# T5-bias attention and a gated adapter layer on one core: loads without a cast, regrouped exps, and a PV tile by head

## The chip, the cores and the metric

The kernel runs on one core of one Trainium2 chip. The metric is device time in microseconds (us) of one execution; lower is better. A core has a matrix engine (PE), whose weight loads are shown as a row of their own (PEld), a vector engine (DVE), a scalar engine for exps (ACT), a general engine (POOL, in code `nc.gpsimd`) and a queue processor (SP, in code `nc.sync`) that here issues transfers (DMAs). Each engine works through its own list of instructions in order; between engines there are semaphore waits. PE writes its results into PSUM, a small memory of eight banks of 2 KB on each of 128 partitions; DVE and ACT read it from there into SBUF, the working memory.

## The reference

Batch 8, 8 heads, 576 tokens, 64 numbers a head. All inputs are f32.

```
scores = q k^T / 8 + bias_table[bucket(|i - j|), head]
attn   = softmax(scores) ;  x = attn v            # x: 4608 tokens x 512
logits = x w_gate                                 # 8 adapters
w      = softmax over the two largest logits
out    = x + sum over these two:  w_e (x A_e) B_e  # A_e 512x16, B_e 16x512
```

The bucket depends on the distance alone and is the last one (31) from distance 128 on.

## The kernel before

**Tokens.** 576 tokens are four blocks of 128 and a tail of 64. Two heads make a pair; there are 8 batches x 4 pairs = 32 pairs, and the main loop (L502) runs over them with five steps g in each. Scores are computed transposed: keys on the partitions, queries along the row. Steps g = 0 to 3 take 128 keys each, for both heads; step 4 takes the 64 tail keys of both heads together.

**Loads.** `load` (L66), `load_tails` and `load_v` issue DMAs from POOL; the source is f32 and the destination bf16, so the transfer itself casts. At the first pair of a batch (L505 to L508) all of the next batch's k and q are asked for, at the second pair its v. The waits for a free buffer stand in POOL's list, as do the memsets of `vts`, `vns` and `tlTs` (L177 to L182, L219 to L222).

**Bias.** Softmax is unchanged by a constant, so the table is taken relative to its last entry, and exp(score + bias) is exp(score) times exp(bias). The factor differs from 1 only where |i - j| < 128. L117 to L149 build exp(bias) as one row per head (`ge`), write it to DRAM, and read it back shifted by one for each partition (`Mr`, `MHr`, L150 to L164); `bias_pair` (L171) copies it reversed into `M` and `MH`. `band` (L278) multiplies the part of the exps near the diagonal with it, on DVE.

**One pair.** `transposes` (L228) puts the pair's k and q through PE and copies them out of PSUM (`kqT`, one DVE copy of 1024 columns); at a batch's first pair also the tails (`tlT`). `qk` (L253) makes 1024 columns of scores for the four query blocks and two heads, and 128 for the tail queries, in three PSUM banks; `softmax_exp` (L272) takes the exp of all 1152 columns in one instruction (640 in step 4). One step later in the list, `pv_main` (L295) and `pv_rest` (L316) multiply the previous pair's exps with v, which has a column of ones so that the sum of exps comes out beside the result: three query blocks in one PSUM tile (`pvA`), the fourth and the tails in another (`pvB`). `norm_main` and `norm_rest` (L341 to L362) divide, on DVE. In the tail rows of `pvB` each half holds one head's queries against both heads' v; `mask` zeroes the half that does not belong.

**The adapter layer.** When a batch's four pairs are done, `pieces` (L477) puts its work into a queue: transposes of x (`m_x`, and `m_xtail` for the tails of two batches together), logits and gates (`m_gate`), x A (`m_z`), its transpose (`m_zT`), the product with B plus x (`m_out`, `m_outt`) and the stores, issued from SP. The main loop takes one piece at the steps 0, 3 and 4 of each pair.

**Order.** It is written out by hand: `manual_schedule` (L54) keeps each engine's instructions in program order. PSUM has two tiles of three banks for scores (`scp`) and two of one bank for all else (`acp`).

The softmax here doesn't subtract the row's maximum and nothing guards it: scores larger than these inputs give would overflow.

## Time and profile before

| | us |
|---|---|
| runs: median (lowest to highest, two runs) | 260.19 (259.83 to 260.55) |
| profiled execution: span, first to last instruction | 257.7 |
| what lies around the span, by the median | 2.5 |
| first exp of the scores starts | 28.63 |
| third pair's first exp starts | 41.20 |
| last pair's first exp starts | 233.96 |
| last exp of the scores starts | 238.37 |

The profile is of one execution. Its page gives each engine's busy time, then the span in 40 slices with the busy tenths of each engine; the trace behind it answers by group of instructions, by tile, by wait and by stretch of time. A group's row reads: line, engine, operation, output <- inputs, shapes, count, then busy time in all and mean ns of one, then the engine's idle time just before them. A row of waits reads: who waited, at which line, for whom, the sum in us, how often, the longest.

### The profile page before, as it was taken

The numbers are of one execution on the slowest core, as the hardware profiler recorded it, in microseconds if no ns is written. First come the engines' busy times: TensorE is split into PE (matmuls) and PEld (weight loads), VectorE is DVE, ScalarE is ACT, GpSimd is POOL, SyncE is SP. The second block draws the span as 40 slices with busy tenths as digits, with TensorE's granted clock in tenths as the row PEclk, the third lists the DMA queues.
The fourth block names the chain that finished last, engine by engine and source line by source line (L and its number), as shares of the span: only waits on it lengthen the run. The fifth ranks groups of instructions, "written<-read, shape, count | busy, mean of one in ns | idle before, by whom it ended". The sixth has DMA issues, their size and how long they took to land.

```text
span 257.7 us, 6522 instructions
## 1 busy us (share of the span) xinstructions
PE 189.7 (74%) x2576; PEld 120.1 (47%) x2576; DVE 205.9 (80%) x641; ACT 165.4 (64%) x174; POOL 117.3 (46%) x155
## 2 busy tenths in 40 slices
PE   0020698797878868897799778987898788888852
PEld 0010255465545655456356554564465544664710
DVE  3200678999898888999979898989998889989972
ACT  2000469897769767886688677867796678868100
POOL 8997999745733591185508560549052000000000
PEclk9999999999999999999889999999999999999965
DMA  4999999969893999399939992799969003202205
GB/s 27 141 154 153 94 131 114 137 42 99 85 201 54 105 84 84 122 146 85 163 95 107 58 142 34 133 166 101 147 109 69 0 3 123 84 3 83 85 21 183
DMA packets 124759, 25.56 MB, mean 99 GB/s; under 512 B 118960, under 2 KB 119992, under 8 KB 124728
## 3 DMA queue, kind: packets, MB, share of 16 engines
q0 software_dynamic: 112768, 14.16, 89.6%
q1 hardware_dynamic: 11960, 10.97, 14.6%
q8 instruction: 20, 0.33, 0.5%
q14 instruction: 11, 0.09, 0.1%
HBM read 29.84 MB, written 9.45 MB: 152 GB/s over the span
## 4 chain that ended last, share of the span: by engine, by line
DVE 50%; PE 26%; ACT 7%; POOL 6%; issue 5%; DMA 3%; ACTq 0%; POOLq 0%; DVEq 0%
PE pvA L310 11%; DVE x L348 6%; PE sc L262 5%; DVE x L360 3%; DVE kqT L250 3%; DMA vn_86<-in_v_dram 3%; DVE o L457 3%; DVE xT L377 3%; PE pvA L304 2%; PE kqps L247 2%; DVE rcA L347 2%; POOL qn L69 2%; DVE rmB L358 2%; PE sc L258 1%; PE dl L455 1%
## 5 line engine op out<-in xcount | busy, mean ns | idle before, releaser
L262 PE MATMUL sc<-kqT 64*128 64x512 bf16 x256 | 51.8, 402 | 0.0
L69 POOL DMA_DIRECT2D kn<-in_k_dram x36 | 31.2, 896 | 19.1 <-PE kqps L247 18.2
L69 POOL DMA_DIRECT2D qn<-in_q_dram x36 | 31.0, 906 | 1.6 <-DMA vn_86<-in_v_dram 1.5
L258 PE MATMUL sc<-tlT_184,kqT 128*128 128x128 bf16 x64 | 14.5, 226 | 18.3 <-DVE kqT L250 13.0
L69 POOL DMA_DIRECT2D vn_87<-in_v_dram x16 | 14.0, 894 | 28.4 <-PE pvB L336 28.4
L69 POOL DMA_DIRECT2D vn_86<-in_v_dram x16 | 14.0, 896 | 27.7 <-PE pvB L336 27.6
L262 PEld LDWEIGHTS <-kqT 64*128 64x128 bf16 x256 | 12.4, 93 | 26.5 <-issue 17.4
L250 DVE COPY kqT<-kqps 128x1024 bf16<-128x1024 bf16 x32 | 21.8, 683 | 3.5 <-PE kqps L247 3.4
L457 DVE TENSOR_TENSOR o<-dl,x 128x512 f32<-128x512 f32 x32 | 21.8, 683 | 1.6 <-DMA out_dram<-o 0.8
L258 PEld LDWEIGHTS <-kqT 128*128 128x128 bf16 x128 | 12.8, 100 | 17.7 <-DVE kqT L250 13.2
L348 DVE TENSOR_TENSOR x<-pvA,rcA 128x384 bf16<-128x384 f32 x32 | 17.8, 557 | 1.1
L455 PE MATMUL dl<-Bb,zT 128*128 128x512 bf16 x32 | 13.3, 421 | 6.8 <-DVE zT L449 2.8
L275 ACT ACTIVATE p_227<-sc 128x1152 bf16<-128x1152 f32 x1 | 1.1, 1131 | 23.4 <-PE sc L262 23.4
L239 DVE COPY tlT_184<-tps 64x512 bf16<-64x512 bf16 x8 | 3.4, 419 | 15.4 <-POOL tlT_184 L221 15.3
L258 PE MATMUL sc<-tlT_186,kqT 128*128 128x128 bf16 x64 | 14.2, 222 | 1.7 <-ACT p_571 L275 0.7
L360 DVE TENSOR_TENSOR x<-pvB,rmB 128x256 bf16<-128x256 f32 x32 | 13.6, 424 | 1.1
L347 DVE RECIPROCAL rcA<-pvA 128x6 f32<-128x6 f32 x32 | 6.2, 195 | 10.1 <-PE pvA L304 9.9
L247 PE MATMUL kqps<-ident,kn 128*128 128x128 bf16 x128 | 13.3, 229 | 1.0 <-DVE o L457 0.6
L412 ACT ACTIVATE ex<-df 128x32 f32<-128x32 f32 (+1 forms) x12 | 2.7, 222 | 17.0 <-DVE df L409 17.0
L234 PE MATMUL tps<-ident,tl 128*128 128x128 bf16 x32 | 3.4, 232 | 13.3 <-DMA tl<-in_q_dram 13.3
L247 PE MATMUL kqps<-ident,qn 128*128 128x128 bf16 x128 | 13.1, 228 | 0.0
L247 PEld LDWEIGHTS <-kn 128*128 128x128 bf16 x128 | 8.2, 101 | 7.5 <-issue 6.8
(1431 smaller groups left out, 655.4 us busy)
## 6 DMA issues: line engine op xcount, KB each, us to landing
out_dram<-o SPq DMA_DIRECT2D x32, 256.0 KB, 2.1
kn<-in_k_dram POOLq DMA_DIRECT2D x28, 128.0 KB, 4.1
qn<-in_q_dram POOLq DMA_DIRECT2D x28, 128.0 KB, 4.7
vn_86<-in_v_dram POOLq DMA_DIRECT2D x16, 128.0 KB, 5.1
vn_87<-in_v_dram POOLq DMA_DIRECT2D x16, 128.0 KB, 4.4
out_dram<-o SPq DMA_DIRECT2D x8, 128.0 KB, 4.6
Mr<-g_d SPq DMA_DIRECT2D x1, 576.0 KB, 6.6
tl<-in_k_dram POOLq DMA_DIRECT2D x8, 64.0 KB, 4.0
```

The lines of the kernel that those rows point to most:

```text
L69: nc.gpsimd.dma_start(out=o, in_=src[b, h0:h1, j * 128:(j + 1) * 128, :] .rearrange("h p d -> p h d"))
L247: nc.tensor.transpose(ps[:, w, j * 128:(j + 1) * 128], n[:, j, 2 * hp:2 * hp + 2, :], ident)
L250: nc.vector.tensor_copy(t, ps)
L258: nc.tensor.matmul(sc[:, 1024:1152], lhsT=t[:, 0, g * 128:(g + 1) * 128], rhs=tt[:, hp, 1, :], start=True, stop=True)
L262: nc.tensor.matmul(sc[:, h * 512:(h + 1) * 512], lhsT=t[s, 0, g * 128:(g + 1) * 128], rhs=t[s, 1, :], start=True, stop=True)
L310: nc.tensor.matmul(acc[:, qb, h, :], lhsT=p[:, o:o + 128], rhs=vn[:, g, 2 * hp + h, :], start=first, stop=False, skip_group_check=True)
L347: nc.vector.reciprocal(rc, acc[:, :, :, D])
L348: nc.vector.tensor_tensor(x[:, 0:3, 2 * hp:2 * hp + 2, :], acc[:, :, :, :D], rc.unsqueeze(3).to_broadcast((128, 3, 2, D)), op=ALU.mult)
L360: nc.vector.tensor_tensor(x[:, 3:5, 2 * hp:2 * hp + 2, :], acc[:, :, :, :D], rm.unsqueeze(3).to_broadcast((128, 2, 2, D)), op=ALU.mult)
L377: nc.vector.tensor_copy(xT[:, :, half * 256:(half + 1) * 256], ps)
L455: nc.tensor.matmul(ps, lhsT=zT[:, t, :], rhs=Bb, start=True, stop=True)
L457: nc.vector.tensor_tensor(o, ps, xs[b][:, t].rearrange("p h d -> p (h d)"), op=ALU.add)
```

## The change

- **Loads** come per pair, in f32, from SP, without a cast: two for k, one for q, two for v. Up to four pairs are asked for ahead. The first pair's q and the bias table are issued from ACT.
- **q** is laid out so that partition p holds tokens 4p to 4p + 3, which makes one run of 1 KB. Query column (j, p) of a tile is now token 4p + j; the output's rows are stored by the same rule. So a key block's band covers 64 or 96 columns in each of the four groups j, and `M` is built with a step of 4.
- **Casts** to bf16 are instructions of POOL (`cast_kq`, `cast_v`, `cast_tail`, `cast_vtail`); for the first pair k and the tails are cast on DVE and q on ACT.
- **Exp groups** are 1024 columns in two banks. The fifth group of a pair holds the tail queries against the four key blocks and the tail keys against the four query blocks; tail queries against tail keys are done once a batch for all four pairs (`tails_sc`, `tails_band`).
- **PV** uses one tile of two banks, one head in each, filled in six parts; it is normalized in one go (`norm`). A third tile pool (`misc_ps`) takes everything else.
- **The order**: scores are issued one group ahead of their exp and the band follows one group behind it; gating is cut into three pieces, `m_z` into two, `m_xtail` runs for each batch; pieces carry weights, and each step of a pair has a budget.

```diff
-    def load(dst, src, b, h0, h1, cols=None):
-        for j in range(4):
-            o = dst[:, j, h0:h1, :D]
-            nc.gpsimd.dma_start(
-                out=o, in_=src[b, h0:h1, j * 128:(j + 1) * 128, :]
-                .rearrange("h p d -> p h d"))
...
+    def load_nat(t, s, i, e):
+        b, hp = divmod(i, HP)
+        for h in range(2):
+            e.dma_start(out=t[:, :, h, :], in_=s[b, 2 * hp + h, 0:S4, :]
+                        .rearrange("(g p) d -> p g d", p=128))
+
+    def load(i, e0=None, e1=None):
+        b, hp = divmod(i, HP)
+        kf = ldp.tile([128, 4, 2, D], FP32, name="kf", tag="kf")
+        qf = ldp.tile([128, 2, 256], FP32, name="qf", tag="qf")
+        load_nat(kf, k, i, e0 or SY)
+        (e1 or SY).dma_start(out=qf, in_=q[b, 2 * hp:2 * hp + 2, 0:S4, :]
+                             .rearrange("h (p j) d -> p h (j d)", j=4))
+        stg[i] = [kf, qf, None]
...
+    def cast_kq(i, e0=None, e1=None):
+        kb = ntp.tile([128, 4, 2, D], BF16, name="kb", tag="kb")
+        qb = ntp.tile([128, 4, 2, D], BF16, name="qb", tag="qb")
+        copy_on(e0 or PL, kb, stg[i][0])
+        copy_on(e1 or PL, qb, stg[i][1].rearrange("p h (j d) -> p j h d", j=4))
+        kq[i] = (kb, qb)
+
+    def cast_v(i, e=None):
+        vn = vns[i % 4]
+        copy_on(e or PL, vn[:, :, :, 0:D], stg[i][2])
...
+    load(0, SY, AC)
     load_tails(0)
...
+    cast_kq(0, DVE, AC)
+    cast_tail(0, DVE)
+    for t in tlTs:
+        PL.memset(t, 0.0)
...
+    M = cp.tile([128, H, 4, 96], BF16, tag="M")
+    MT = cp.tile([128, H, 64], BF16, tag="MT")
+    MH = cp.tile([128, HP, 4, 32], BF16, tag="MH")
+    MHT = cp.tile([128, HP, 2, 64], BF16, tag="MHT")
...
+    def bias_pair(hp, e):
+        e.tensor_copy(M[:, 2 * hp:2 * hp + 2],
+                      rev(Mr, 2 * hp, 383, [[MW, 2], [-1, 4], [-4, 96]]))
...
+    load(1)
     load_v(0)
-    load_kq(0, 2, H)
...
+    load_vtails(0)
+    load_bias(2, H)
+    load_v(1)
+    load(2)
+    load_v(2)
+    load(3)
+    load_v(3)
...
         else:
-            nc.tensor.matmul(sc[:, 0:512], lhsT=tt[:, hp, 0, :], rhs=t[:, 1, :],
+            for g in range(4):
+                nc.tensor.matmul(sc[:, g * 128:(g + 1) * 128],
+                                 lhsT=t[:, 0, g * 128:(g + 1) * 128],
+                                 rhs=tt[:, hp, 1, :], start=(g == 0), stop=True,
+                                 skip_group_check=True)
+            nc.tensor.matmul(sc[:, 512:1024], lhsT=tt[:, hp, 0, :], rhs=t[:, 1, :],
                              start=True, stop=True)
...
+        pm = p.rearrange("p (h j q) -> p h j q", h=2, j=4)[:, :, :, q0:q1]
+        DVE.tensor_tensor(pm, pm, M[:, 2 * hp:2 * hp + 2, :, x0:x0 + q1 - q0],
+                          op=ALU.mult)
...
+        if part == 0:
+            a = acp.tile([128, 2, S4], FP32, name="pv", tag="pv")
+            st[(i, "acc")] = a[:, :, 0:5 * D1].rearrange("p h (s d) -> p h s d", s=5)
...
+        rc = sp.tile([128, 2, 5], FP32, name="rc", tag="rc")
+        DVE.reciprocal(rc, acc[:, :, :, D])
+        DVE.tensor_tensor(x[:, :, 2 * hp:2 * hp + 2, :].rearrange("p s h d -> p h s d"),
+                          acc[:, :, :, :D],
+                          rc.unsqueeze(3).to_broadcast((128, 2, 5, D)), op=ALU.mult)
...
+    BUD = (.6, .1, .2, .1, .2)
     for i in range(NPAIR + 1):
         b, hp = divmod(i, HP)
...
+        live = i < NPAIR
+        for c in range(5):
+            nxt = (i, c + 1) if c < 4 else (i + 1, 0)
+            if live:
+                if nxt[0] < NPAIR:
+                    sc[nxt] = qk(*nxt)
+                softmax_exp(i, c, sc.pop((i, c)))
+            prev = (i, c - 1) if c else (i - 1, 4)
...
+            if i < HP and c == 1:
+                bias_pair(i, DVE)
+            if (0, 0) <= prev and prev[0] < NPAIR and (live or c == 0):
+                band(*prev)
+            if live:
+                if c == 0:
+                    if i + 4 < NPAIR:
+                        load(i + 4)
+                    if i + 2 < NPAIR:
+                        cast_kq(i + 2)
...
+            if i > 0:
+                for pt in {1: (0, 1), 2: (2,), 3: (3, 4), 4: (5,)}.get(c, ()):
+                    pv(i - 1, pt)
+            if c == 2 and i + 1 < NPAIR:
                 transposes(i + 1)
-            if g == 1 and i > 0:
-                acc = pv_main(i - 1)
-                norm_main(i - 1, acc)
-            if g == 2 and i > 0:
-                acc = pv_rest(i - 1)
-                norm_rest(i - 1, acc)
+            if i > 0 and c == 4:
+                norm(i - 1)
                 if i % HP == 0:
                     queue += pieces(i // HP - 1)
-            if g in (0, 3, 4) and i > 0 and queue:
-                queue.pop(0)()
...
```

## The prediction

> **What bounds the kernel now.** I read the head of the page first, then the busy time of each engine between two marks, then the waits.

> ```profile
> span 257.7 us, 6522 instructions
> ...
> PE 189.7 (74%) x2576; PEld 120.1 (47%) x2576; DVE 205.9 (80%) x641; ACT 165.4 (64%) x174; POOL 117.3 (46%) x155
> ...
> DVE  3200678999898888999979898989998889989972
> ...
> ```

> The marks are the first exp of the third pair (41.20) and of the last pair (233.96). Busy times by engine between them:

> ```profile
> 41.20:234.00 192.80, 162.37 (x2305) 104.61 (x2304) 174.29 (x537) 148.16 (x156) 79.36 (x97) 0.99 1.01 95
> ```

> The columns are PE, weight loads, DVE, ACT, POOL, granted clock, DMA share, GB/s. This is 29 pairs at 6.65 us, and DVE works 174.29/29 = 6.01 us of each. It is the engine that sets the pace; ACT needs 5.11 of it. The list of waits says what fills the other 0.64, and what the first 28.6 us are:

> ```profile
> DVE rcA L347 <- PE pvA L304: 9.9, 25, 1.4
> ...
> ACT p_227 L275 <- PE sc L262: 23.4, 1, 23.4
> ...
> DVE tlT_184 L239 <- POOL tlT_184 L221: 15.3, 1, 15.3
> ```

> At the start, DVE waits 15.3 us for a memset of `tlT` that stands in POOL's queue behind the loads' issues, with the operands' transposes done at 14.8 (the timeline). So the time is 41.2 (to the third pair) + 192.8 + 23.7 (last pair's own exps and the serial end) = 257.7; the median of the runs is 260.19, 2.5 above the span, which I add at the end.

> **The change part by part.**

> *The start.* POOL no longer issues loads, so the memset is early. What is late next, in order: SP issues four loads from 0.74 (about 0.5 each), and the last, the tails, lands 4.0 later (the row of `tl`): 7. DVE casts them (at most 0.68, its time for 512 f32), then runs the ladder of bias copies, now behind that cast: 2.2 us of rows (0.48, 0.23, 0.34, 0.27, 1.22 less overlap), 9.9. Three `tlT` copies (1.28), `kqT` (0.68), scores (0.6): first exp near 12.5, where it was 28.6. The bias table goes on: exp (0.63), write out (1.44, from 5.25 to 6.69 in the timeline), so `Mr` is asked for at 12. SP holds every later load behind this wait and the two `MHr` issues (1.34): pair 1's loads start at 13.8 and land at 18, two casts (0.66 each), transposes, copy and scores (1.9) give pair 1 at 21. Ten issues and then pair 2's own three, at 0.55, end at 21; landing, casts and the same 1.9 give pair 2's first exp near 27.5. Before: 41.2. DVE stands at the first `M` copy until `Mr` lands (12 + 3.9 = 15.9); behind it in its queue is only work that needs pair 1's operands, so this costs nothing. Gain 13.7; if loads land in 2.3 (the 32 KB row) pair 2 starts at 25, if in 6.6 (`Mr`'s) at 32.

> *Norm.* One tile for both heads: five instructions become two.

> ```profile
> L348 DVE TENSOR_TENSOR x<-pvA,rcA 128x384 bf16<-128x384 f32 x32 | 17.8, 557 | 1.1
> L360 DVE TENSOR_TENSOR x<-pvB,rmB 128x256 bf16<-128x256 f32 x32 | 13.6, 424 | 1.1
> L347 DVE RECIPROCAL rcA<-pvA 128x6 f32<-128x6 f32 x32 | 6.2, 195 | 10.1 <-PE pvA L304 9.9
> L356 DVE RECIPROCAL rcB<-pvB 128x4 f32<-128x4 f32 x32 | 5.6, 176 | 0.2
> L358 DVE TENSOR_TENSOR rmB<-rcB,mask 128x4 f32<-128x4 f32 x32 | 5.2, 162 | 1.1
> ```

> Read the means: 195 + 557 + 176 + 162 + 424 = 1514 ns a pair. From 256 to 384 elements costs 133 ns, so 640 take 424 + 3 x 133 = 824, and ten reciprocals 235: 1059. **-0.455 us a pair.**

> *Bands.* The same elements in six instructions: 413 + 549 + 549 + 413 + 2 x 215 = 2.35, where the three lines took (55.72 + 6.29 + 8.15)/29 = 2.42: -0.07. The tails of four pairs are multiplied in one 512-element operation: +0.41/4 = +0.10.

> *Gating.* `m_xtail` runs for each batch with two 256-element copies (285 each, between the 213 and 424 rows) in place of one of 679 per two batches: +0.06 a pair. `m_z` in halves: 2 x 424 for 680, +0.04. The rest is the same. DVE then has 6.01 - 0.455 - 0.07 + 0.10 + 0.06 + 0.04 = **5.69 us a pair**. The bias tables, now read with a step of 4, cost four copies of 0.75 (the 768-element `MH` copy took 0.72) for 0.5 and three of 512 elements (0.42 to 0.68) for 0.95: +2 us, once.

> *POOL casts beside DVE.* Per pair three casts of 512 elements (0.60 to 0.66, the weight casts) and a quarter of three for the tails: 3.75 casts, 2.3 us. POOL has room; the question is DVE. The timeline holds one meeting:

> ```profile
> 36.40 0.60 POOL L214 CAST Bb<-B_f 128x512 bf16<-128x512 f32 x1
> 36.49 0.80 DVE L289 TENSOR_TENSOR p_282<-p_282,M 128x512 bf16<-128x512 bf16 x1
> ```

> The band took 796 ns, not 413: it ran until 0.29 after the cast's end. Hence 0.38 a meeting. Bounds: nothing, and every cast meets a band, 3.75 x 0.38 = 1.43 a pair. Bands are 39% of DVE's work, so I take 0.39 x 1.43 = 0.55, less what falls in time that DVE would idle: **+0.4**. [...]

> *Exp groups.* Starts of successive exps lie 1.02 apart at 1152 columns and 0.72 at 640, so 1024 columns take 0.91; five and a quarter of a 512-column one: 4.7 us a pair where it was 4.8. It hides under DVE as before.

> *PE.* 50 PV matmuls a pair for 41; 24 of them in a row took 0.71 us (120.50 to 121.21), so +0.27, less about as much in scores. PE waits for ACT and DVE now and has cover for it. Scores are issued one group ahead and bands one group late, so that DVE should find its operands ready: of 0.64 idle (0.33 of it for PV) I leave **0.2**; bounds 0 and 0.64.

> *Loads.* Per pair SP issues 5 loads, a tail load and 1.2 stores. A load may wait for the one eight before it, and stores wait for DVE with later loads behind them, but loads run four pairs ahead. Prices:

> ```profile
> L206 SPq DMA_DIRECT2D A_f<-in_moe_A_dram x4: 540/1414/2413, 9.2 to 14.5; - x4
> ...
> L460 SPq DMA_DIRECT2D out_dram<-o x32: 327/332/356, 67.4 to 252.9; - x32
> ```

> A load with 512 rows of 256 B lies between a store of 128 rows (0.33) and the quickest `A_f` with 1024 (0.54): 6 x 0.5 + 1.2 x 0.35 = 3.4 us a pair, under 6.3. Bytes: 0.86 MB in, 0.29 out in 6.3 us, 183 GB/s; between 9 and 16 us the trace moved 185. [...] No row here shows such plain loads. [...]

> *The sum.* Pair: 5.69 + 0.4 + 0.2 = 6.3. Span: 27.5 + 29 x 6.3 + 2 + 23.5 (the end: one norm after all of PV, +0.7, no wait for an output buffer, -0.8) = 235.7; plus 2.5: **238**.

> **Rivals.**

> 1. *Little contention* (22%): POOL's casts, released by transposes and PV, fall beside DVE's PSUM copies. Pair 5.8, start 26: 26 + 168 + 2 + 23 + 2.5 = 222. For it: POOL busy only a third. Against: DVE has few gaps to absorb a meeting.
> 2. *Each cast meets a band* (10%): pair 5.69 + 1.43 + 0.1 = 7.2, 264; the start pays for the loss and no change can be told.
> 3. *The load queue becomes the bound* (9%), the slower case. Its place is SP: if an issue takes `A_f`'s 1.41 us, as with a full queue, 6 x 1.41 + 0.4 = 8.9 us a pair, and 27.5 + 258 + 2 + 23.5 + 2.5 = 313. It decides from 7.07 us a pair, that is 1.1 us per load. For it: `A_f` itself, and 8 loads in flight at most, which at 4.5 us each is 0.56 a load. Against: those issues shared the engines with POOL's packets (89.6% of 16 engines' span), which go away.
> 4. *Only the start is gained* (14%): handoffs between PE, ACT and DVE keep the pair at 6.65: 27.5 + 193 + 2 + 23.5 + 2.5 = 248.

> **How the numbers follow.** The forecast, 230 to 246, has 45%. Range 220 to 258: it takes in cases 1 and 4, about half of case 2's weight beyond the upper end and most of case 3 stay out. A change of 2% (5.2 us) is about what can be told here: faster is below 255. Forecast, 1 and 4 and a little of 2: 0.83; same 0.08; slower 0.09.

> **What would show it.** First exp near 12 to 14 and the third pair's near 27; DVE busy 5.7 to 6.2 a pair with the norm at about 825 ns; some bands at 0.7 to 1.0 us wherever a POOL cast overlaps, 413 or 549 elsewhere; SP never the last releaser of a cast after the first four pairs. Wrong if POOL's casts wait for DMA in the middle, if plain 256 B loads land late, if bands with runs of 64 or 96 elements are slower than before, or if PE holds ACT while waiting for a gating copy.

## The result and the profile after

The changed kernel takes **272.0 us** (271.94 to 272.05) where the kernel before took 260.2: a ratio of **1.047** (95% interval 1.040 to 1.053). It is slower by 4.7%; the forecast was 238, with a range up to 258. The profiled execution took 271.94 with a span of 270.1. Times are medians of all executions of a kernel, while ratios leave out executions more than 1.5% above the fastest of the same kernel, so the two do not always divide exactly.

The head of the page of the changed kernel, with the busy times and the slices of DVE and of the granted clock:

```profile
span 270.1 us, 7307 instructions
...
PE 200.9 (74%) x2872; PEld 139.5 (52%) x2872; DVE 210.2 (78%) x568; ACT 163.8 (61%) x183; POOL 79.6 (29%) x143
...
DVE  1537745887797989896989879898988699869772
...
PEclk9999975997999899986999689988999599979955
```

DVE's total rose by 4 us although 73 of its instructions are gone, and its share of the span fell: more work and more waiting. The last row is new. This is the same row of the kernel before:

```profile
PEclk9999999999999999999889999999999999999965
```

There the clock of PE stood at 9 (90% or more of full speed) nearly throughout the loop; in the changed kernel a notch of 5 to 8 returns about once a batch. The first slices of this row are not readings: the trace has no clock record before 38.3 us (before) and 30.6 us (changed), and up to there two score matmuls take 0.61 us, later, at the full clock, 0.39. So PE ran slow at the start of both kernels although the row shows 9.

To compare like with like I take 24 pairs, from the first exp of the fifth pair to that of the 29th. Busy times by engine between these marks, first of the kernel before, then of the changed one (columns as in the prediction: PE, weight loads, DVE, ACT, POOL, clock, DMA share, GB/s):

```profile
52.56:213.71 161.15, 136.06 (x1929) 87.52 (x1929) 145.24 (x453) 122.61 (x130) 70.47 (x86) 0.99 1.04 97
```

```profile
47.52:221.71 174.19, 141.92 (x2155) 101.36 (x2155) 151.07 (x400) 120.91 (x136) 56.00 (x93) 0.91 0.61 158
```

Divided by 24, a pair took 6.71 us before and takes 7.26 now; DVE works 6.05 and 6.29 of it and is idle 0.66 and 0.96. The span against the sum of the prediction:

| stretch | predicted | measured | difference |
|---|---|---|---|
| start to the third pair's first exp | 27.5 | 28.8 | +1.3 |
| third and fourth pair, with the bias tables | 14.6 | 18.8 | +4.2 |
| 24 pairs | 151.2 | 174.2 | +23.0 |
| 29th to 31st pair | 18.9 | 22.6 | +3.7 |
| from the last pair's first exp | 23.5 | 25.8 | +2.3 |
| span | 235.7 | 270.1 | +34.4 |

Of the 23.0, 151.07 - 24 x 6.09 = 4.9 are DVE's work, and the other 18.1 its idle time, 0.96 a pair where 0.2 was written down.

Who waits, in the list of waits of the changed kernel over the whole span (waiting engine and line, releaser, us in all, times, longest), ACT first:

```profile
ACT p L321 <- PE sc L306: 30.7, 34, 7.2
ACT p L321 <- PE sc L315: 26.9, 19, 4.0
ACT ex L441 <- DVE df L431: 25.3, 12, 7.2
```

```profile
PE sc L306 <- ACT p L321: 19.5, 12, 3.5
PE xps L392 <- DVE x L379: 8.3, 8, 1.2
...
PE tps L264 <- POOL tl L115: 6.5, 1, 6.5
PE dl L489 <- DVE zT L483: 4.1, 5, 1.0
PE kqps L292 <- POOL kb L115: 3.9, 2, 2.8
```

ACT's wait for `df` in the kernel before, between 52 and 234 us:

```profile
ACT ex L412 <- DVE df L409: 10.3, 10, 1.3
```

`ex` is the gating exp. It waits for DVE's `df` (17.7 us of the 25.3 fall between 47.5 and 244), which stands behind a norm and the logits' copy in DVE's list; the exps of the scores are queued behind it on ACT, and PE finds no free score buffer. The timeline at one such place shows both sides, ACT and then PE (start, us, engine, line, operation, how often, and in brackets the idle time before it):

```profile
148.24 0.23 ACT L441 ACTIVATE ex<-df 128x32 f32<-128x32 f32 x1 [1.75 <-DVE df L431]
150.21 0.21 ACT L441 ACTIVATE ex<-df 128x8 f32<-128x8 f32 x1 [1.74 <-DVE df L431]
150.33 1.92 ACT L321 ACTIVATE p<-sc 128x1024 bf16<-128x1024 f32 x2
```

```profile
146.54 0.39 PE L306 MATMUL sc<-kqT 64*128 64x512 bf16 x2
147.21 0.65 PE L351 MATMUL pv<-vn,p 128*128 128x65 bf16 x16 [0.27 <-DVE lg L426]
151.38 0.61 PE L306 MATMUL sc<-kqT 64*128 64x512 bf16 x2 [3.52 <-ACT p L321]
```

PE stands 3.52 us, and after it the same two score matmuls take 0.61 us instead of 0.39. Two stretches of 6.8 us, by window, show the clock in and behind this place:

```profile
150.10:156.90 6.80, 5.52 (x58) 4.27 (x58) 4.54 (x16) 4.24 (x6) 2.40 (x4) 0.50 0.63 150
156.90:163.70 6.80, 6.31 (x102) 4.36 (x99) 6.38 (x16) 5.18 (x6) 1.99 (x3) 1.00 0.01 4
```

The granted clock was 0.50 in the first and 1.00 in the second: 58 matmuls against 102, and DVE worked 4.54 us against 6.38. Part of that is its wait for PE: the `rc` of a norm waited 1.65 us for PE's `pv`, until 157.2.

The fourth pair has a wait of its own. SP's queue and PE in the timeline:

```profile
27.70 4.04 SPq L244 DMA_DIRECT2D A_f<-in_moe_A_dram  x4
...
32.95 1.07 SPq L76 DMA_DIRECT2D vf<-in_v_dram  x2
```

```profile
41.77 0.61 PE L264 MATMUL tps<-ident,tl 128*128 128x128 bf16 x4 [6.48 <-POOL tl L115]
```

The weights' issues stand in SP's list ahead of the tail loads of batch 1, which are issued only at 36.9 and 37.6; POOL's cast of them ends at 41.7, and PE has stood at their transposes since 35.3, with all later scores behind. ACT waited 7.16 us.

### The profile page after: what moved, and what is told of

Same layout as the page of the kernel before. It is cut to its first block, busy times and chain, and to the rows that moved or that the text cites. A ratio compares the mean times of both kernels' runs of the same rounds, so it can differ in the third digit from the quotient of the medians.

```text
span 270.1 us, 7307 instructions
## 1 busy us (share of the span) xinstructions
PE 200.9 (74%) x2872; PEld 139.5 (52%) x2872; DVE 210.2 (78%) x568; ACT 163.8 (61%) x183; POOL 79.6 (29%) x143
## 4 chain that ended last, share of the span: by engine, by line
PE 42%; DVE 36%; issue 5%; SPq 5%; ACT 5%; DMA 4%; POOL 1%; ACTq 0%; DVEq 0%; POOLq 0%
PE pv L351 9%; PE sc L306 9%; DVE p L336 7%; DVE x L379 7%; PE kqps L292 5%; ACT p L321 4%; DVE o L491 4%; DVE kqT L295 3%; PE pv L367 3%; SPq L76 3%; PE xps L392 3%; DMA tf<-in_q_dram 3%; DVE rc L378 2%; PE zp L464 2%; PE pv L359 2%
## 5 line engine op out<-in xcount | busy, mean ns | idle before, releaser
L321 ACT ACTIVATE p<-sc 128x1024 bf16<-128x1024 f32 x160 | 155.3, 1023 | 61.3 <-PE sc L306 30.7
L306 PE MATMUL sc<-kqT 64*128 64x512 bf16 x256 | 54.6, 423 | 22.4 <-ACT p L321 19.5
L336 DVE TENSOR_TENSOR p<-p,M 128x512 bf16<-128x512 bf16 (+1 forms) x128 | 65.7, 545 | 1.1 <-ACT p L321 0.2
L351 PEld LDWEIGHTS <-p 128*128 128x128 bf16 x1024 | 44.1, 104 | 24.2 <-issue 12.8
L351 PE MATMUL pv<-vn,p 128*128 128x65 bf16 x1024 | 52.3, 203 | 4.0 <-DVE x L379 2.9
L115 POOL CAST kb<-kf 128x512 bf16<-128x512 f32 x31 | 21.1, 680 | 85.8 <-PE kqps L292 38.2
L295 DVE COPY kqT<-kqps 128x1024 bf16<-128x1024 bf16 x32 | 22.0, 687 | 14.5 <-PE kqps L292 13.8
L379 DVE TENSOR_TENSOR x<-pv,rc 128x640 bf16<-128x640 f32 x32 | 26.4, 824 | 1.1
L115 POOL CAST vn<-vf 128x512 bf16<-128x512 f32 x32 | 20.9, 654 | 16.0 <-PE pv L359 15.1
L115 POOL CAST qb<-qf 128x512 bf16<-128x512 f32 x31 | 20.5, 660 | 3.0 <-DMA qf<-in_q_dram 2.3
L441 ACT ACTIVATE ex<-df 128x32 f32<-128x32 f32 (+1 forms) x12 | 2.7, 222 | 25.3 <-DVE df L431 25.3
L292 PE MATMUL kqps<-ident,kb 128*128 128x128 bf16 x128 | 14.8, 249 | 3.9 <-POOL kb L115 3.9
L378 DVE RECIPROCAL rc<-pv 128x10 f32<-128x10 f32 x32 | 6.9, 217 | 10.8 <-PE pv L367 10.6
L292 PE MATMUL kqps<-ident,qb 128*128 128x128 bf16 x128 | 15.0, 251 | 0.3 <-POOL qb L115 0.2
L359 PE MATMUL pv<-vn,p 128*128 128x65 bf16 x256 | 14.7, 203 | 0.0
```

Source lines behind the costliest of these rows:

```text
L115: e.tensor_copy(o, i)
L292: nc.tensor.transpose(ps[:, w, j * 128:(j + 1) * 128], kq[i][w][:, j], ident)
L295: DVE.tensor_copy(t, ps)
L306: nc.tensor.matmul(sc[:, h * 512:(h + 1) * 512], lhsT=t[s, 0, c * 128:(c + 1) * 128], rhs=t[s, 1, :], start=True, stop=True)
L321: AC.activation(p, sc, ACT.Exp, scale=scale)
L336: DVE.tensor_tensor(pm, pm, M[:, 2 * hp:2 * hp + 2, :, x0:x0 + q1 - q0], op=ALU.mult)
```

## The experiments

Three suspects, then: **A**, the wait for the gating exp, with the clock that falls behind it; **B**, POOL's casts, which lengthen DVE's work; and the tails behind the weights. Ratios are to the kernel before, run beside each. Kernels with half-speed stretches scatter between executions (e6 from 256.4 us at a clock of 0.938 to 263.6 at 0.901), and each profile is of one of them: 263.3 us in e5, 261.5 in e6 and 244.5 in e11, above the median, and 265.8, 264.1 and 276.3 in e1, e2 and e3, below it. So a difference of about 0.1 us between two pairs of this table tells nothing: the loops of e1 and e5 differ only in where the weights are cast, and their pairs are 7.07 and 7.18.

| | casts | gating exp | PE filled | pair | DVE busy | DVE idle | PE busy | clock | ratio (95%) |
|---|---|---|---|---|---|---|---|---|---|
| before | in the DMA | same step | | 6.71 | 6.05 | 0.66 | 5.67 | 0.99 | 1 |
| after | POOL | same step | | 7.26 | 6.29 | 0.96 | 5.91 | 0.91 | 1.047 (1.040 to 1.053) |
| e1 | POOL | later | | 7.07 | 6.34 | 0.72 | 5.71 | 0.95 | 1.038 (1.032 to 1.044) |
| e2 (tails) | POOL | same step | | 7.12 | 6.41 | 0.72 | 5.67 | 0.94 | 1.022 (1.015 to 1.030) |
| e3 | POOL, k and q twice | same step | | 7.43 | 6.80 | 0.63 | 5.71 | 0.93 | 1.074 (1.066 to 1.083) |
| e4 | POOL | same step | in part | 7.29 | 6.33 | 0.96 | 5.99 | 0.95 | 1.047 (1.040 to 1.053) |
| e5 (tails) | POOL | later | | 7.18 | 6.48 | 0.70 | 5.70 | 0.95 | 1.004 (1.000 to 1.008) |
| e6 (tails) | in the DMA | same step | | 7.19 | 5.84 | 1.35 | 5.81 | 0.92 | 0.995 (0.990 to 1.000) |
| e7 (tails) | in the DMA | later | | 6.47 | 5.83 | 0.64 | 5.40 | 1.00 | 0.950 (0.944 to 0.956) |
| e9 (tails) | in the DMA | same step | yes | 6.81 | 5.82 | 0.99 | 5.94 | 0.98 | 0.964 (0.960 to 0.967) |
| e12 | POOL | same step | yes | 6.89 | 6.30 | 0.59 | 5.86 | 1.00 | 1.007 (1.004 to 1.010) |
| e13 (tails) | POOL | later | yes | 7.16 | 6.43 | 0.73 | 6.14 | 0.99 | 1.021 (1.016 to 1.025) |

Pair, busy and idle are us per pair over the 24 pairs of each profile, from rows like the two above. "(tails)" marks the kernels in which the tails of batch 1 no longer wait behind the weights. e8, e10, e11 and e14 are told below.

### One suspect at a time: e1 to e4

**e1** moves the gating exp.

```diff
-        l.append((0, lambda: m_gate2(km, 4)))
+        l.append((-1, lambda: m_gate2(km, 4)))
```

> Edit: the gating exp of a batch (m_gate2, L441) goes into the step after its logits (m_gate1) instead of the same step; nothing else. Theory A, the gate chain: in the changed kernel ACT stands at ex for DVE's df (25.3 us over 12, of it 7.2 at the end), the next exps of the scores are queued behind it, PE then waits 2.0 to 3.5 us at its next score matmul once a batch, and right behind each of these gaps the granted clock is 0.5 for 3.4 or 6.8 us. The pair in which this falls takes 9 to 11 us where its neighbours take 6.5. A expects the ex waits in the loop to fall from 18 to under 4 us, PE's gaps over 2 us gone from the loop, the clock near 1.0 there, and 2.5 to 4 us less in each of seven batches: 272 to about 250 (244 to 256). Theory B, DVE is the bound and POOL's casts lengthen its bands (625 and 465 ns for 549 and 413): the wait only moves, and the time stays above 265.

Measured 268.7 us, 1.038. The intervals of this and of the changed kernel overlap; the gain is 2 or 3 us, not 22. PE's longest gap at the scores in the loop fell from 3.5 to 1.5 us and DVE's idle time to 0.72, but DVE's work did not shrink, and half-speed stretches still occur, behind other gaps (`ztps` waiting for `zt`, 1.7 to 1.9 us). Theory A in the form that I gave it falls (it expected 250); B alone does not explain it either, since the pair is still 0.72 above DVE's work.

**e2** moves the weights.

```diff
-                    if i == 0:
+                    if i == 2:
                         load_weights()
...
-                    if i == 1:
+                    if i == 3:
                         cast_weights()
```

> Edit: the adapter weights are loaded at the third pair and cast at the fourth, in place of the first and second, so that the tail loads of batch 1 stand in SP's list ahead of them. In the changed kernel PE stood 6.48 us at the transposes of these tails (from 35.29), with the cast waiting for a load that SP issued at 36.9 to 38.3, behind 4.04 us of A_f issues; ACT stood 7.16 us, and the clock was 0.5 for 10.2 us from 37.5 on. Theory A expects this wait gone and the half-speed stretch with it: 6 to 9 us less, about 265. Theory B (DVE bound by contention) expects the work that waits here to be caught up later: less than 3 us.

Measured 265.7 us, 1.022: by 2.4% of the time before, 6.3 us, below the changed kernel. The fifth pair begins at 43.1 instead of 47.5. The wait was a loss of its own.

**e3** doubles a part of POOL's casts.

```diff
-        copy_on(e0 or PL, kb, stg[i][0])
-        copy_on(e1 or PL, qb, stg[i][1].rearrange("p h (j d) -> p j h d", j=4))
+        for _ in range(2 if e0 is None else 1):
+            copy_on(e0 or PL, kb, stg[i][0])
+            copy_on(e1 or PL, qb, stg[i][1].rearrange("p h (j d) -> p j h d", j=4))
```

> Edit: POOL casts k and q of each pair twice (the same cast again), so POOL has 31 x 2 more casts of about 0.62 us, 38 us in all, that read and write SBUF beside DVE's bands. Theory B (POOL's casts beside DVE are what the time is lost to) expects DVE's busy time to rise by another 0.2 us a pair or more and the time by 6 us or more: 278 or above. Theory A (the gate chain and the clock) expects DVE's busy time to rise as much, but most of it to vanish in DVE's idle time: 0 to 4 us, 272 to 276.

Measured 279.9 us, 1.074: by 2.8% of the time before, 7.2 us, above the changed kernel, as B expected. DVE's work rose by 0.51 us a pair, of which 0.34 went into its idle time. Groups of the changed kernel, then of e3, over the whole span:

```profile
L336 DVE TENSOR_TENSOR p<-p,M 128x768 bf16<-128x768 bf16 x64 | 40.0, 625 | 0.6 <-ACT p L321 0.2
L336 DVE TENSOR_TENSOR p<-p,M 128x512 bf16<-128x512 bf16 x64 | 29.7, 465 | 0.4
L379 DVE TENSOR_TENSOR x<-pv,rc 128x640 bf16<-128x640 f32 x32 | 26.4, 824 | 1.1
```

```profile
L337 DVE TENSOR_TENSOR p<-p,M 128x768 bf16<-128x768 bf16 x64 | 43.0, 673 | 0.4
L337 DVE TENSOR_TENSOR p<-p,M 128x512 bf16<-128x512 bf16 x64 | 35.8, 560 | 0.4
L380 DVE TENSOR_TENSOR x<-pv,rc 128x640 bf16<-128x640 f32 x32 | 26.4, 824 | 1.1
```

The bands, with two SBUF inputs, grow from 549 and 413 (before) to 625 and 465 and with more casts to 673 and 560; the norm, whose input is in PSUM, stays at 824 in both.

**e4** keeps the wait and gives PE work in it.

```diff
-        first = True
-        for t in range(t0, t1):
+        for _ in range(4 if nt == 4 and t0 == 0 else 1):
+            first = True
+            for t in range(t0, t1):
...
```

> Edit: the first half of m_z for each batch's 512-token part issues its eight matmuls four times, each time starting the sum anew, so the result is the same; the three extra rounds are about 1.5 us of PE work that stands where PE now waits for ACT (117.95 to 120.01, for one). The wait of ACT for the gating chain stays. If the half-speed clock after each gap is what makes the 9 to 11 us pairs, PE does not go idle for long, the clock stays near 1.0 in most batches, and the time falls by 2 to 3 us a batch: 252 to 260. If the wait alone costs the time and the clock only marks it, the time stays within 2 us of 272, or rises by up to 1 us a batch.

Measured 271.4 us, 1.047: by its expectation the clock only marks the wait. But the edit missed its place in half of the batches. Where two gating exps follow each other, this work comes behind the gap; gaps of 2.9 to 3.7 us and the half-speed stretches stayed there, and the extra work then ran at half speed. As a whole the experiment decides nothing, and e9 and e12 below do it again with the work in the right place. But where it hit, in the other half of the batches, it shows the same as they do: the 7th, 15th and 23rd pairs, which took 6.56, 7.66 and 6.55 us in the changed kernel, took 5.38, 5.07 and 5.39 here.

### Two at a time: e5, e6, e7

**e5** is e1 and e2 together.

> Edit: the two edits of order together (the gating exp one step later, the weights after the tails of batch 1). Alone they gave 268.7 and 265.7 for 272.0. If the two losses are separate, as their places in the trace say (one in each batch from the second on, one at 35 us), the sum is 272.0 - 3.3 - 6.3 = 262.4. If DVE's work is the bound and fills any gap, the second edit adds under 2 us: 264 to 266.

Measured 261.4 us, 1.004: as the two losses added.

**e6** takes POOL's casts away (`load_v_cast` and `load_tails_cast`, for v and the tails, are written in the same manner; the pool of `kb` and `qb` gets six buffers for three, and v is asked for two pairs ahead instead of four):

```diff
+    def load_kq_cast(i):
+        b, hp = divmod(i, HP)
+        kb = ntp.tile([128, 4, 2, D], BF16, name="kb", tag="kb")
+        qb = ntp.tile([128, 4, 2, D], BF16, name="qb", tag="qb")
+        load_nat(kb, k, i, PL)
+        PL.dma_start(out=qb, in_=q[b, 2 * hp:2 * hp + 2, 0:S4, :]
+                     .rearrange("h (p j) d -> p j h d", j=4))
+        kq[i] = (kb, qb)
...
-                        load(i + 4)
-                    if i + 2 < NPAIR:
+                        load_kq_cast(i + 4)
+                    if i + 2 < 4:
                         cast_kq(i + 2)
```

> Edit: from the fifth pair on (and for the tails from batch 1 on) POOL issues loads that cast on the way, as before the change; POOL's casts are gone from there, everything else is as in the changed kernel. The tails of batch 1 no longer stand behind the weights in SP's list, so the 7 us wait at 36.7 goes too. Theory B (POOL's casts lengthen DVE's bands, and DVE is the bound): bands back at about 549 and 413 ns, 128-element ones at 215, gating operations at 190, DVE's busy time per pair from 6.29 to about 5.8, and the time at 272 - 29 x 0.5 - 6.5 = 251. Theory A (gate chain and clock): the operations are as short, but ACT's wait for df, PE's gaps and the half-speed stretches stay, and the time falls by the 6.5 us of the tails alone: 265.

Measured a ratio of 0.995 (ten executions, median 261.0 us). This is the surprise. DVE's work fell from 6.29 to 5.84 us a pair, as B said, and the pair stayed at 7.19 in the profiled execution: the 0.45 turned into idle time, 1.35:

```profile
39.24:211.71 172.47, 139.47 (x2130) 101.38 (x2154) 140.13 (x401) 120.95 (x135) 127.49 (x157) 0.92 1.15 102
```

In this execution most of the gain over the changed kernel is the wait at the tails: the fifth pair begins at 39.2, 8.3 us earlier, and the 24 pairs are 1.7 us shorter.

**e7** has the casting loads and both edits of order.

> Edit: the casting loads and both edits of order. Both theories now add up: DVE at 5.8 us a pair and 0.7 of idle time give 6.5, third pair at 28.5: 28.5 + 29 x 6.5 + 26 + 2.5 = 245.5. If POOL's issues (0.7 to 0.9 us each before the change, 6 a pair: about 5 us of 6.5) become late, PE waits for DMA at the transposes and it stays near 255.

Measured **245.6 us, 0.950**, within 0.1 us of the expectation. The stage of the same 24 pairs:

```profile
39.93:195.31 155.38, 129.69 (x2130) 91.35 (x2153) 140.01 (x402) 120.74 (x135) 124.74 (x156) 1.00 1.24 110
```

The pair is 6.47, the clock 1.00. From the fifth pair on, neither edit alone moved the pair by more than 0.2 us (7.26 to 7.07, to 7.19), and both moved it by 0.79. The ratios say the same without leaning on single profiles. In e2, e5, e6 and e7 the tails no longer wait, and the ratios are 1.022, 1.004 with the exp later, 0.995 with casting loads and 0.950 with both: 1.8% and 2.7% alone, 7.2% together. I read this as two limits at nearly the same height, DVE's lengthened work and the chain from the gating exp over ACT to PE, each of which hides what the removal of the other would bring; how much of it is the clock, the next runs show.

### The clock by itself: e9 and e12

Both put matmuls into PE's list where it waits; nobody reads their result, and the wait of ACT stays.

```diff
     def m_gate3(key, nt):
+        if nt == 4:
+            fill = msp.tile([128, 512], FP32, name="fill", tag="ms")
+            for _ in range(8):
+                nc.tensor.matmul(fill, lhsT=Ab[:, 0, :], rhs=xT_of(key)[:, 0, :],
+                                 start=True, stop=True)
```

**e9**, on e6:

> Edit of the kernel with casting loads (gating exp still in the step of its logits): eight matmuls of 512 columns, about 1.7 us, whose result nobody reads, stand in PE's list at each batch's m_gate3, which is where PE waits 2.05 us for ACT. The wait of ACT for the gating chain is as before. With casting loads the pair took 7.19 us from the fifth to the last, DVE busy 5.84 of it, granted clock 0.92; with the gating exp moved as well 6.47, 5.83 and 1.00. If the clock that falls to 0.5 after the gap is most of that difference: clock at 0.98 or more, the pair at 6.7 or less, the time 10 us or more below the 258.9 (0.995 of before) of that kernel, 249. If it is ACT standing still with the exps behind it: clock up, the pair at 7.0 or more, within 4 us of 258.9.

Measured 250.3 us, 0.964, where e6 had 0.995: 3.1% of the time before. The pair fell from 7.19 to 6.81, about half of the 0.72 us that separate e6 from e7. So the clock is about half of that difference, as far as single profiles tell; for the rest, DVE still idles 0.99 us a pair where e7 has 0.64, with ACT's wait for `df` as it was (22.4 us, 22.5 in e6).

**e12**, on the changed kernel itself:

> Edit of the changed kernel itself, and nothing else: the eight matmuls whose result nobody reads at m_gate3. POOL's casts, the gating exp and the tails behind the weights stay. The pair took 7.26 us from the fifth to the last, DVE busy 6.29, granted clock 0.91. If the clock is most of the loss here too, as with casting loads (258.9 to 250.3): clock at 0.97 or more behind 48 us, the pair near 6.8 (DVE's 6.29 and 0.5 of idle time), 272 - 29 x 0.4 = 260. If, with POOL's casts, DVE's lengthened work is the bound by itself: 266 or above.

Measured **260.3 us, 1.007**: 4.0% of the time before, 10.4 us, below the changed kernel, by work that does nothing. The clock, the stage of the same 24 pairs and the waits of ACT in e12:

```profile
PEclk9999975999999999999999999999999999999997
```

```profile
46.73:212.05 165.32, 140.55 (x2202) 96.37 (x2201) 151.08 (x401) 120.49 (x135) 58.98 (x93) 1.00 0.64 166
```

```profile
ACT p L321 <- PE sc L306: 29.5, 28, 6.9
ACT ex L441 <- DVE df L431: 25.8, 12, 7.2
ACT p L321 <- PE sc L315: 17.1, 20, 4.0
```

The wait for `df` is as long as it was (25.3). What went is the notches in the clock, except the one behind the tails, and with them a third of what ACT waits at L315. DVE's work is the same to 0.01 us (151.08 for 151.07), the pair fell from 7.26 to 6.89, and 29 x 0.37 = 10.7 is the gain. So A was right about the clock and I had tested the wrong half of it in e1: moving the exp closes PE's largest gap, but other gaps remain behind which the clock falls (e1 and e5, with POOL's casts, still have four and five half-speed stretches between 48 and 225 us; e7, without them, has one).

### What POOL's casts cost: e13

**e13** is e5 with PE filled (six such matmuls at `m_gate3`, six at `m_zT`).

> Edit of the kernel with POOL's casts and both edits of order: PE gets six matmuls of 512 columns whose result nobody reads at m_gate3 and six at m_zT of each batch's 512-token part, the places where it waited 1.2 to 1.8 us, so that the clock stays up with POOL's casts in place. The casting loads then differ from it by the casts alone. If POOL's casts cost what they add to DVE's work (0.45 to 0.65 us a pair: 5.84 to 6.29, 5.83 to 6.48) whenever DVE is the bound: the pair at 7.0, the time at 0.9498 x 259 + 29 x 0.55 = 262, as without the filling (1.004). If they cost it mainly through the gaps that they make on PE, and so through the clock: 250 to 254.

Measured 263.7 us, 1.021, with the clock at 0.99. Against e7 (0.950) the pair is longer by 0.69, and DVE's work by 0.60 of it. But e13 is also 1.7% slower than e5, although its clock is higher: here filling has a price of its own, and DVE waited 6.5 us, 0.2 a pair, for the transposes behind the filling at `m_zT`. So 0.69 is not the cost of the casts alone. The shortest pair with POOL's casts is e12's 6.89, 0.42 above e7; with the order mended the casts cost something near these figures, and no run isolates it. Between e12 and e9, where the gating exp stays in its old place, the same casts cost 0.08 us a pair: there DVE idles 0.99 without them, which takes them in.

### The start of the kernel before: e8

```diff
     make_identity(nc, ident)
+    tlTs = []
+    for i in range(2):
+        t = cp.tile([128, HP, 3, 128], BF16, name=f"tlT{i}", tag=f"tlT{i}")
+        nc.gpsimd.memset(t, 0.0)
+        tlTs.append(t)
```

> Edit of the kernel before, nothing of the change: the two memsets of tlT go ahead of the other memsets and loads in POOL's list. That is the part of the start that the change repairs by taking the loads off POOL. The tails' transposes were done at 14.8 there and DVE waited until 25.8 for the memset; the first exp came at 28.6. Expected: first exp near 17; the second pair's operands are loaded some 3 us later than before, so that it begins near 28 and the third near 36: 5 us less, 255. If the loads of the second and third pair are the bound (v and k, q of the other pairs are issued until 27), nothing is gained: 260.

(The lines of their old place further down go.) Measured 258.7 us, 0.997 (0.994 to 1.001): no difference. The first exp came at 17.1 as expected, the next one only at 29.6, the third pair at 40.7 (41.2 before): PE waited 7.2 us for the second pair's k, which is still issued behind v. The loads were the bound and the memset had hidden it; the start that the change gains is worth what it is because the loads moved.

### A version that beats both: e10, e11, e14

**e10** adds to e7 that a batch's pieces enter the queue one step later and that the second pair's transposes come one step later.

```diff
-            if c == 2 and i + 1 < NPAIR:
+            if c == (3 if i == 0 else 2) and i + 1 < NPAIR:
                 transposes(i + 1)
             if i > 0 and c == 4:
                 norm(i - 1)
-                if i % HP == 0:
-                    queue += pieces(i // HP - 1)
...
+            if i > 0 and c == 4 and i % HP == 0:
+                queue += pieces(i // HP - 1)
```

> Edit of the kernel with casting loads and both edits of order: a batch's pieces enter the queue one step later, so that the transposes of x (m_x) do not stand right behind norm in PE's list, where PE waits 1.0 us in each batch; and the second pair's transposes go one step later in the first pair, behind the scores of its last group. Expected: PE's waits at xps (8.1 us over 8) and DVE's at xT (4.4) gone, 0.5 to 1 us in each of seven batches, and 1 to 2 us at the start, where ACT waited 4.0 us: 245.6 - 6 = 240. If DVE's work fills the gap, under 2 us: 244.

Measured 245.4 us, 0.944 (0.940 to 0.949), not told apart from e7. The waits at `xps` went (8.1 to 3.3 us) and the pair fell to 6.40, but the first pair took 13.87 us instead of 9.27: DVE's copy of the second pair's `kqT` then stands behind the bias copy that waits for `Mr`.

**e11** leaves the second pair's transposes where they were.

> Edit: the kernel with casting loads and both edits of order, and a batch's pieces one step later; the second pair's transposes stay where they were. Moving those as well cost the first pair 4.6 us (13.87 for 9.27), because DVE's copy of kqT then stood behind the bias copy that waits for Mr, and the later batches gained about as much: 24.2 and 27.2 us a pair of batches for 25.3 and 26.9. Expected: the start as with both edits of order (fifth pair near 40), the batches as with the pieces later: 245.6 - 3 = 242 to 243. If the pieces one step later only move DVE's work into the next pair, 245 to 246.

Measured **241.1 us, 0.931 (0.928 to 0.934)**: faster than both kernels; the pair is 6.34, DVE's work 5.77. **e14** adds five filling matmuls at `m_zT` to it.

> Edit of the kernel with casting loads, both edits of order and the pieces one step later: five matmuls whose result nobody reads at m_zT, where PE waited 1.1 us in every second batch and after which the clock was 0.5 for 3.4 us (pairs of 8.8 us for 6.6). If the clock is what makes these pairs long: 8.8 falls to about 7 in three or four batches, 241 - 6 = 235 to 236. If they are long for DVE's work, 240 to 241.

Measured 240.0 us, 0.928 (0.922 to 0.934), not told apart from e11. Two half-speed stretches are left in the loop, and the pairs of 8.8 us became 7.75, not 7: DVE now waits 3.3 us in all at `zT` for the transposes behind the filling, where it was 0.6 in e11.

## Why the prediction was wrong

The sign was wrong, and one term carries most of it.

- **Idle time, the step that failed.** Of 0.64 us of idle time I left 0.2, because scores are issued one group ahead, and of PE I wrote that it "waits for ACT and DVE now and has cover for it". It was 0.96. No row stood behind the 0.2: the lowest of any kernel here is 0.57 (e11), 0.1 under the kernel before. And PE had no cover. The gating exp is put into ACT's list in the step of its logits, behind which ACT stands 18 us in the loop. The wait exists in the kernel before too (10.3 us), and I had not asked what stands behind it in the new order: before, no gap of PE in the loop was longer than 1.2 us, here 2.0 to 3.5 follow it, and then the clock. The 0.37 us a pair that e12 shows for the clock is nearly half of the error of 0.76 in the idle time. Of the 23.0 us over 24 pairs that makes 8.9 for the clock and 4.9 for DVE's work; the other 9.2 are idle time that stays when the clock is up, and that I had written off without a row. What fills it no run takes apart.
- **The clock** is in no step and in no rival. I took the durations of PE's work from the kernel before as given, and its row was at 9 in nearly all of the loop.
- **The start.** First exp at 11.0 (12.5 predicted), third pair at 28.8 (27.5; bounds 25 to 32): right. But the load step listed the loads of pairs and left `load_weights` out of SP's list, with the tails of the next batch behind it; e2 puts that at 6.3 us. I had used the issues of those weights as a price only; here four of them took 4.04 us.
- **Norm.** 217 + 824 = 1041 ns for 1059: right, the product to the nanosecond.
- **DVE's other work.** 5.83 us a pair without casts (e6, e7) for 5.69. Small.
- **Casts beside DVE.** +0.4 predicted, 6.29 - 5.84 = 0.45 measured; 0.6 with the order mended. Right in size. In the changed kernel's trace, bands that meet a cast are longer by 0.2 us (512 elements: 625 ns on average over 15, 415 without; 768 elements: 733 over 26, and 551) rather than 0.38, but more operations than these meet one: the 128-element bands (343 over 16, 216 without) and the gating's operations on 32 elements (423 to 633, 184 to 192 without) too. All of these have two inputs in SBUF. What had an input in PSUM did not lengthen: the norm took 824 beside a cast and without, the sum `o` 676 and 683; nor did the gating's reduction and reciprocal, with a single input (187 and 178 beside a cast, 186 and 178 without, two meetings each). On average a meeting cost a 512- or 768-element band a third of a 0.63 us cast. In the one meeting in the prediction the band did not stand still until the cast's end: 413 ns begun there would have ended 0.41 us after it, and it ended 0.29 after.
- **The order of limits.** The sum took DVE as the only bound of the pair. With that, removing 0.45 us of casts should have been worth 10.8 us over the 24 pairs, and those of e6 show 1.7.
- **Rivals.** None came to pass. The load queue (rival 3) was not the bound: a load's issue took 0.5 us. POOL's casts did wait for DMA in the middle, which I had listed as a way to be wrong: 33.8 us at `kb` in all, 20.1 of it in three waits in the loop. PE waited for POOL's `kb` twice (3.9 us), both at the start, so in the loop those waits cost nothing. Rival 2 had the right period, 7.2, for another reason: DVE's work was 6.29 of it and not 7.1. Rival 4 kept the idle time of before; no rival let it grow.
- **The end.** 25.8 for 23.5, with PE at half speed from 256 on.

## What to carry to other kernels

An instruction that waits for another engine's chain belongs one step further down its own in-order queue (e7 against e6: 0.950 for 0.995); ask what is queued behind it, and who waits for that. Write down idle time only from a row, and when one limit is taken away compute the next one before the gain is booked: here two edits worth at most 0.2 us a pair each were worth 0.8 together. Read the granted clock with the gaps of PE, and test a suspicion by giving PE work that does nothing at that place: a few lines show what the clock costs (10.4 us in e12), as long as nothing on the bounding engine waits behind them (in e13 DVE waited 6.5 us).
